# Splitting the last batch's gates from its last step, regrouping the logits as six and two batches, and moving the last splits to VectorE

## Chip, cores and metric

The kernel runs on one core of a Trainium2 chip. The metric is device time in microseconds (us) of one execution, lower is better. Engines are TensorE (PE, with its weight loads PEld), VectorE (DVE), ScalarE (ACT), GpSimd (POOL) and SyncE (SP, which only issues transfers here).

## What is computed

An FFT filter on x of 8 batches, 2496 positions, 256 channels, and then a mixture of 8 experts on its 19968 tokens. Each (token, expert) pair is taken in order of falling logit; a token goes to the first expert that still has room (2496 places each).

```python
X = np.fft.rfft(x, axis=1)
y = np.fft.irfft(X * (filt_r + 1j * filt_i)[None], n=2496, axis=1)
x = y.reshape(8 * 2496, 256)
logits = x @ w_gate                      # 8 experts
for idx in np.argsort(-logits.flatten()):
    tok, e = int(idx) // 8, int(idx) % 8
    if assigned[tok] >= 0 or counts[e] >= cap:
        continue
    assigned[tok] = e; counts[e] += 1
for e in range(8):
    out[assigned == e] = np.maximum(x[assigned == e] @ w1[e], 0) @ w2[e]
```

## The kernel before, in words

**Forward part, batch by batch.** `run` writes a list of steps by hand, each with a slot (ten slots to a batch) and a priority within the slot, sorts it and emits the steps in that order. A scheduler then orders each engine's queue from that: earlier emission goes first where it is ready by the scheduler's own model. `s1` and `s2` are the two forward steps; `s2(b, g, dh)` (L224) multiplies with the filter, two products on VectorE (L235, L236) and the sum on GpSimd (L237, L238), into a tile P. Five groups g make up a batch.

**Two uses of P.** `tr(b, q)` (L240) transposes half a group on TensorE (L248) for the way back to positions, and splits the result in a high part (ScalarE, L269) and a low part (L270, VectorE). For the last batch and q over 4 it only copies the transposed rows to the spare tile `y7` (L250); their split comes later, in `inv1` (L290), with the subtraction on GpSimd. In its odd steps `tr` also multiplies the group with the gate's weights (16 small matmuls, L257) and copies the result to `vs` (L259, one buffer). `inv1(b, q)` (L286) is the first inverse step: six matmuls, a copy and two transfers to `zd` (L298; for the last two batches from ScalarE's queue).

**The logits.** They take a short cut through the inverse, eight columns to a batch. `trv` transposes `vs` and splits it into `Vh` and `Vl` (L276 to L279); `v1(g, b0, b1)` is the first inverse step on the columns of batches b0 to b1 (12 matmuls and a copy, L316 and L318); `v2` makes 22 transposes and copies (L332, L333); `v3` multiplies and copies to `lg` (L342, L344). This is done twice: for batches 0 to 6 together and, once its last group is there, for batch 7. `prep` (L523) makes seven VectorE operations of the logits: maximum, a mask Gm, the best expert, and the indicator matrix A (L534).

**Routing.** `threshold` searches the first expert to fill by counting in 11 rounds. A round is a comparison on VectorE (L550, not in the first round), 11 to 13 count matmuls (L558), three VectorE operations (L566 to L568), one matmul (L571) and a few small operations. After the last round come the places of the tokens, and the indices with which tokens are gathered.

**The way back.** The second inverse step, `inv2_parts` (L376), is done for the first two batches while the forward part runs, and for the other six as 30 units after it. A unit is two or five groups of 256 columns: matmuls (L391), ScalarE copies (L392), one transfer to `xs` (L395). In `emit`, `after` is a generator that interleaves these units with `inv1` of q from 5 to 9 of the last batch; TensorE's queue there is written out in program order, and `Pump` puts the count matmuls between the units by planned costs and due times. The first count (L558) is emitted before the loop. `more_z` and `more_z2` load ahead into tiles that the forward part has freed.

**Experts.** A last copy releases the weights' load (L993, L795); tokens are gathered from `xs` (L811), transposed (L825), and go through two matmul stages per expert (L847, L890). Routing for the later experts is interleaved there.

Of the kernel before, what the change touches and what calls it, by code (L numbers as in the profile page):

```python
# [7 lines left out]
F32, F32R = mybir.dt.float32, mybir.dt.float32r  # L8
# [4 lines left out]
B, N, D, E8, FF = 8, 2496, 256, 8, 1024  # L13

N1, N2, K1, J = 39, 64, 20, 64
G = 22
S = B * G
# [9 lines left out]
V1, V1D, V2, V3, VP, AC = 8, 0.5, 3, 2, -1, 6.5  # L27
# [106 lines left out]
class Fft:  # L134
# [105 lines left out]
    def tr(s, b, q):  # L240

        nc = s.nc
        g, k = q // 2, 2 * (q % 2)
        yt = [s.yt[b, g, dh] for dh in range(2)]
        p = s.ps.tile([128, 2, D], F32, name="pa", tag="c", bufs=4)
        for h in range(2):
            for dh in range(2):
                nc.tensor.transpose(p[:, h, 128*dh:128*dh+128], yt[dh][:, k+h], s.id)  # L248
        if b == B - 1 and q > 4:
            nc.scalar.copy(s.y7b(q), p)  # L250
        else:
            s.split(b, q, p, nc.vector)
        if k:
            p = s.ps.tile([128, 128], F32, name="pv", tag="c", bufs=4)
            for dh in range(2):
                for k in range(4):
                    nc.tensor.matmul(p[32*k:32*k+32], s.gate[:, dh], yt[dh][:, k], start=dh == 0, stop=dh == 1, skip_group_check=True)  # L257
            s.vs[b, g] = s.wp.tile([128, 128], F32, name="vs", bufs=1)
            nc.scalar.copy(s.vs[b, g], p)  # L259

    def y7b(s, q):
        if q == 9 and s.y9 is None:
            s.y9 = s.wp.tile([128, 4, 128], F32, name="P", bufs=NP).rearrange("p k d -> p (k d)")
        y = s.y7[:, 80+512*q:592+512*q] if q < 9 else s.y9
        return y.rearrange("p (k d) -> p k d", d=D)

    def split(s, b, q, v, eng):
        y = s.yd[b, q] = [s.wp.tile([128, 2, D], F32R, name=n, bufs=3) for n in ("yh", "yl")]
# [17 lines left out]
    def inv1(s, b, q):  # L286

        nc = s.nc
        if (b, q) not in s.yd:
            s.split(b, q, s.y7b(q), nc.gpsimd)  # L290
        zt = s.wp.tile([128, 2, D], F32, name="zt", bufs=ZB)
        p = s.ps.tile([128, 2, D], F32, name="pa", tag="c", bufs=4)
        for h in range(2):
            s.inv(p[:, h], 2*q + h, [y[:, h] for y in s.yd[b, q]])
        last = b == B - 1
        (nc.scalar.copy if last else s.cps[q % 2])(zt, p)
        for r in range(2):
            (nc.scalar if b >= B - 2 else nc.sync).dma_start(s.zd[b].rearrange("a n c -> n a c")[:N2, 20*r+2*q:20*r+2*q+2], zt[64*r:64*r+64])  # L298
# [5 lines left out]
    def v1(s, g, b0, b1):  # L304

        nc = s.nc
        if s.y7 is None:
            s.y7 = s.wp.tile([128, K1 * D], F32, name="Y1", tag="Y1", bufs=2)
            nc.gpsimd.memset(s.y7[:72, :2640].rearrange("p (a n) -> p a n", n=3*G)[:, :, N2:], 0.0)
        c = 8 * (b1 - b0)  # L310
        r = slice(64, 64 + c) if b0 else slice(0, c)
        p = s.pt([128, 4, 128], not b0)
        for k in range(4):
            (h, l), (Eh, El) = ([t[:, 4*g+k] for t in ts] for ts in ((s.Vh, s.Vl), s.cE))
            for m, (v, w) in enumerate(((h, Eh), (h, El), (l, Eh))):
                nc.tensor.matmul(p[:c, k], v[:, 8*b0:8*b1], w, start=m == 0, stop=m == 2)  # L316
        z = s.y7[r, :2640].rearrange("p (r k n) -> p k r n", r=2, k=K1)[:, 4*g:4*g+4, :, :N2]
        nc.scalar.copy(z, p[:c].rearrange("p k (r n) -> p k r n", r=2))  # L318

    def v2(s, b0, b1):  # L320

        nc, c = s.nc, 8 * (b1 - b0)
        r = slice(64 if b0 else 0, (64 if b0 else 0) + c)
        s.U = s.zp.tile([120, G, c], F32, name="xo", tag="xo", bufs=2)
        n = 8 if c > 8 else G
        for g0 in range(0, G, n):
            g1 = min(g0 + n, G)
            p = s.pt([128, g1 - g0, c], not b0)
            for g in range(g0, g1):
                a = s.y7[r, g:g+1]  # L330
                z = bass.AP(tensor=a.tensor, offset=a.offset, ap=[list(a.ap[0]), [G, 6 * K1]])
                nc.tensor.transpose(p[:120, g-g0], z, s.id[r, r])  # L332
            nc.vector.tensor_copy(s.U[:, g0:g1], p[:120])  # L333

    def v3(s, b0, b1):

        nc, c = s.nc, 8 * (b1 - b0)
        n = 8 if c > 8 else G
        for g0 in range(0, G, n):
            g1 = min(g0 + n, G)  # L340
            p = s.pt([128, g1 - g0, c], not b0)
            s.lastv = nc.tensor.matmul(p[:120], s.cD, s.U[:, g0:g1], start=True, stop=True).ins  # L342
            with s.tc.issue_after(s.lastq):
                nc.vector.tensor_copy(s.lg[:, b0:b1, g0:g1], p[:117].rearrange("p g (b e) -> p b g e", e=8))  # L344

    def more_z(s, units):

# [50 lines left out]
    def run(s, cp, wp, xp, ps, freed, prep, rest):  # L398
# [11 lines left out]
        for b in range(B):  # L410
            o = 10*b
# [5 lines left out]
            for g in range(5):  # L417
                for dh in range(2):
                    at(o + 2*g + dh, 1, s.s2, b, g, dh)
                at(o + 2*g + 4.5, 3.5, s.trv, b, g)  # L420
            for q in range(10):
                at(o + q + 3, 3, s.tr, b, q)
                if b < B - 1 or q < 2:
# [5 lines left out]
                    at(z, 5, s.inv2, b, t)  # L429
        at(10*B - 9.5, 0, freed)  # L430
        for g in range(5):
            at(10*B - V1 + g*V1D, 3.8, s.v1, g, 0, B - 1)
            at(10*B - 5.2 + 2*g, 3.6, s.v1, g, B - 1, B)
        at(10*B - V2, 3.8, s.v2, 0, B - 1)
        def prep0():
            with s.tc.issue_after(s.lastq):
                prep(0, G * (B - 1))
        at(10*B - 0.9, 3.7, s.v3, 0, B - 1)
        at(10*B - VP, 3.8, prep0)
        def act():  # L440
            s.cps = (s.nc.scalar.copy,) * 2
        at(10*B - AC, 0, act)
# [1 line left out]
            at(10*B - 15, 9, s.load_z, *u)  # L444
        at(10*B - 0.8, 9, s.more_z, rest[3+NZ:9+NZ])
        at(10*B + 2.9, 3.61, s.more_z2, rest[9+NZ:3+NZ+MZ])
        at(10*B + 2.9, 3.6, s.v2, B - 1, B)
        at(10*B + 2.9, 3.62, s.v3, B - 1, B)
        at(10*B + 2.9, 3.64, prep, S - G, S)
        for q in (2, 3, 4):  # L450
            at(10*B + 2.9, 3.7 + 0.01 * q, s.inv1, B - 1, q)
        for e in sorted(ev, key=lambda e: e[:3]):
            e[3](*e[4])

# [6 lines left out]
class Route:  # L461
# [75 lines left out]
    def counts(s, nj, thr, made=False):  # L537


        nc, n = s.nc, s.n  # L540
# [14 lines left out]
        last = (S - 1) // b  # L555
        for k in range(last + 1):
            w = min(b, S - b*k) * n
            nc.tensor.matmul(c[:KL, :w], s.Gm[:, K*k:K*k+KL], s.A[:, b*n*k:b*n*k+w], start=k == 0, stop=k == last, skip_group_check=True)  # L558
        t1 = s.wp.tile([128, 128], F32, name="t1", bufs=2)[:K, :b*n].rearrange("p (e s) -> p e s", s=b)
        D1 = s.wp.tile([128, 8], F32, name="D1", bufs=2)[:K, :n]  # L560
        XT = s.XT[nj].pop(0)
# [350 lines left out]
def emit(tc, i, out):  # L912
    nc = tc.nc
    with ExitStack() as st:
# [67 lines left out]
        with tc.issue_after(f.lastv):  # L982
            while pump.kind != 'X':
                pump.step_main()
        with tc.manual_schedule(engines={mybir.EngineType.PE}):
            while (0, 0) not in pump.tags:
                pump.feed(0.1)
                c = next(units, None)
                pump.feed(c if c else 0.8)
            for c in units:  # L990
                pass
# [18 lines left out]
        n = 0  # L1010
# [110 lines left out]
```

## Time and profile before

| | us |
|---|---|
| median of 3 runs | 1425.95 (1424.56 to 1429.34) |
| profiled execution | 1424.91 |
| its span, first to last instruction | 1423.1 |
| TensorE busy | 1378.7 (97%) |
| VectorE busy | 892.1 (63%) |
| ScalarE busy | 673.4 (47%) |
| GpSimd busy | 486.0 (34%) |
| mean granted clock of TensorE | 0.989 |

A matmul's end is modelled, so a busy TensorE may still be waiting in part; busy time of an engine does not hold its transfer issues. The profile names an instruction by its line, its engine and "out<-in" in the program's tile names: `pv`, `pa`, `rt` are PSUM tiles, `xo` and `Y` hold results of the way back, `zt` and `zd` the first inverse step.

### The profile page before, as it was taken

To read this page: it belongs to the slowest core of one execution; us is meant where nothing else is said; L and a number is where in the kernel's file an instruction comes from. 1 tells how busy PE (TensorE), PEld (TensorE's weight loads), DVE (VectorE), ACT (ScalarE), POOL (GpSimd) and SP (SyncE) were. 2 spreads that over 40 slices of the span, in tenths; PEclk is the share of its full clock that TensorE was granted. 3 is DMA by queue.
4 is the path that set the end of the run, shared out by engine and by line. 5 is a ranking of instruction groups with operands and counts; after the bars stand their busy time and mean duration, and the time that the engine had idled before them with its cause. 6 is when DMAs were issued, how large, how long until landed. Compare 5 with 4: busy or idle time off the path is not lost. (4 is left out here: it accounts for less than half of the span.)

```text
span 1423.1 us, 27225 instructions
## 1 busy us (share of the span) xinstructions
PE 1378.7 (97%) x10338; PEld 1210.5 (85%) x10338; DVE 892.1 (63%) x2548; ACT 673.4 (47%) x1638; POOL 486.0 (34%) x538
## 2 busy tenths in 40 slices
PE   9999999998969999999999999999999999999998
PEld 8898898876538898988889888889898899899988
DVE  5577676775647769658667875876867635423231
ACT  6766666644564246235335534533623635423231
POOL 3443343431034126323422622433433323323312
PEclk9999999999979999999999999999999999999999
DMA  9786675658981022112112212112111321111100
GB/s 376 253 237 179 198 216 137 152 127 241 333 304 57 21 86 77 32 33 94 59 32 82 70 40 82 53 43 98 51 38 49 124 70 51 47 42 51 40 20 29
DMA packets 58701, 153.75 MB, mean 108 GB/s; under 512 B 10954, under 2 KB 32074, under 8 KB 54986
## 3 DMA queue, kind: packets, MB, share of 16 engines
q1 hardware_dynamic: 29920, 70.10, 16.2%
q0 software_dynamic: 18416, 60.37, 13.0%
q10 hardware_dynamic: 10233, 21.53, 4.6%
q8 instruction: 82, 1.34, 0.4%
q14 instruction: 50, 0.40, 0.1%
HBM read 88.32 MB, written 63.70 MB: 107 GB/s over the span
## 5 line engine op out<-in xcount | busy, mean ns | idle before, releaser
L890 PE MATMUL py<-w1h,hl 128*128 128x256 f32 x2496 | 485.8, 287 | 1.0 <-DVE hl L858 0.7
L890 PEld LDWEIGHTS py<-w1h,hl 128*128 128x128 f32 x2496 | 403.0, 191 | 7.2 <-issue 3.2
L890 PE MATMUL py<-w1l,hl 128*128 128x256 f32 (+1 forms) x1280 | 359.6, 283 | 0.0
L901 POOL DMA_INDIRECT out<-y,oid x160 | 168.4, 1052 | 507.5 <-ACT y L900 459.2
L853 ACT ACTIVATE hl<-pz 128x512 fp32r<-128x512 f32 (+1 forms) x320 | 187.1, 587 | 226.7 <-PE pz L847 203.4
L847 PE MATMUL pz<-xo,w0h 128*128 128x512 f32 (+1 forms) x640 | 263.9, 412 | 3.4 <-DVE hl L855 1.8
L855 DVE SCALAR_TENSOR_TENSOR hl<-pz,hl 128x512 fp32r<-128x512 f32 x256 | 175.2, 688 | 144.7 <-ACT hl L853 143.3
L847 PE MATMUL pz<-z,w0h 128*128 128x512 f32 (+1 forms) x640 | 248.7, 389 | 0.0
L847 PE MATMUL pz<-xo,w0l 128*128 128x512 f32 (+1 forms) x640 | 248.4, 388 | 0.0
L890 PEld LDWEIGHTS py<-w1l,hl 128*128 128x128 f32 (+1 forms) x1280 | 241.7, 189 | 1.9
L811 POOL DMA_INDIRECT xg<-xs,xid x160 | 170.1, 1063 | 129.8 <-issue 51.5
L900 ACT COPY y<-py 128x256 f32<-128x256 f32 x152 | 56.6, 372 | 306.3 <-PE py L890 268.0
L847 PEld LDWEIGHTS pz<-xo,w0l 128*128 128x128 f32 x640 | 120.8, 189 | 24.0
L847 PEld LDWEIGHTS pz<-xo,w0h 128*128 128x128 f32 x640 | 121.6, 190 | 22.0 <-DVE hl L855 2.3
L847 PEld LDWEIGHTS pz<-z,w0h 128*128 128x128 f32 x640 | 121.6, 190 | 15.7 <-DVE z L829 0.6
L219 ACT COPY Y<-p 64x240 f32<-64x240 f32 (+1 forms) x302 | 115.2, 381 | 30.4 <-PE p L213 22.4
L237 POOL TENSOR_TENSOR P<-P 128x256 f32<-128x256 f32 x80 | 58.6, 732 | 168.8 <-DVE P L235 168.6
L550 DVE TENSOR_TENSOR Gm<-M,thr 117x1232 bf16<-117x1232 f32 (+2 forms) x80 | 104.4, 1315 | 0.2
L213 PE MATMUL p<-cS,xr 117*128 117x120 f32 x688 | 94.2, 277 | 2.7 <-ACT Y L219 1.5
L213 PEld LDWEIGHTS p<-cS,xr 117*128 117x128 f32 x688 | 86.0, 193 | 6.8 <-ACT Y L219 4.3
L229 PE MATMUL p<-cW,Y 128*128 128x128 f32 x640 | 88.8, 277 | 0.6 <-DVE Q L236 0.6
L229 PEld LDWEIGHTS p<-cW,Y 128*128 128x128 f32 x640 | 80.1, 191 | 5.8 <-issue 3.9
(218 smaller groups left out, 1982.4 us busy)
## 6 DMA issues: line engine op xcount, KB each, us to landing
z<-zd SPq DMA_DIRECT2D x26, 600.0 KB, 5.3
zd<-zt SPq DMA_DIRECT2D x120, 128.0 KB, 2.7
xs<-xo ACTq DMA_DIRECT2D x18, 600.0 KB, 10.0
xr<-x SPq DMA_DIRECT2D x6, 1536.0 KB
xr<-x SPq DMA_DIRECT2D x6, 1216.0 KB, 9.2
zd<-zt ACTq DMA_DIRECT2D x40, 128.0 KB, 3.3
xs<-xo SPq DMA_DIRECT2D x8, 600.0 KB, 6.6
xr<-x SPq DMA_DIRECT2D x8, 512.0 KB, 6.6
```

Of the source, the lines that this page charges most:

```text
L213: s.lastmm = nc.tensor.matmul(p[:, q-q0, :120], xv[:, q-24*h], s.cS1, start=True, stop=True).ins
L219: c = (nc.vector.tensor_copy if (t == 5 if b else cp) else nc.scalar.copy)(dst, src)
L229: nc.tensor.matmul(p[:, k], s.Y1[b][:, 4*g+k, dh*128:dh*128+128], s.cW[:, 4*g+k], start=True, stop=True)
L237: nc.gpsimd.tensor_tensor(P[:, :, :64], P[:, :, :64], P[:, :, 64:], op=OP.subtract)
L550: nc.vector.tensor_tensor(Gm[:, s0:s1, :m], s.M[:, s0:s1].unsqueeze(2).to_broadcast([117, s1 - s0, m]), thr[:117].unsqueeze(1).to_broadcas ...
L811: s.lastg = s.nc.gpsimd.indirect_dma_start(out=xg[:n], out_offset=None, in_=s.xs, in_offset=bass.IndirectOffsetOnAxis(ap=ids[0][:n, t:t+1] ...
L847: nc.tensor.matmul(p[:, :n], w[:, sl], x[:, k, :n], start=m == 0, stop=m == 5)
L853: s.lasta = nc.scalar.activation(h[:, :n], p[:, :n], AF.Relu).ins
L855: s.R.low = nc.vector.scalar_tensor_tensor(l[:, :n], p[:, :n], 0.0, h[:, :n].bitcast(F32), op0=OP.max, op1=OP.subtract).ins
L890: nc.tensor.matmul(p[:a.stop-a.start], hs[g][f][:, a], b[:, 256*f:256*f+256], start=m == 0, stop=m == 8 * len(terms) - 1, skip_group_check ...
L900: s.lasta = nc.scalar.copy(y, p).ins
L901: st = nc.gpsimd.indirect_dma_start(out=out_rows, out_offset=bass.IndirectOffsetOnAxis(ap=ids[1][:w, 4*g+t:4*g+t+1], axis=0), in_=y[:w], i ...
```

## The change

The gates' matmuls and copy leave `tr` and become a step of their own, `gates`. For batches 0 to 6 it is still called in `tr`; for batch 7 it has slots of its own, nearer to `s2`, and three buffers for `vs` in a free part of `y7`; its `trv` follows half a slot later. The logits are grouped as batches 0 to 5 and batches 6 and 7, and all steps of the second group have earlier slots. `v3` copies the first group on ScalarE and waits no longer behind the last `s2`. `prep` of the first group has an earlier slot. `inv1` of q 2 to 4 moves from behind the last logits to ahead of `v2`. The split's subtraction for q from 5 on moves from GpSimd to VectorE, and the splits of q 5, 6 and 7 are emitted right after the last `prep`. The first unit (with `inv1` of q 5) is put behind the first count's last matmul on TensorE.

```diff
@@ in tr, after the split @@
-        if k:
-            p = s.ps.tile([128, 128], F32, name="pv", tag="c", bufs=4)
-            for dh in range(2):
-                for k in range(4):
-                    nc.tensor.matmul(p[32*k:32*k+32], s.gate[:, dh], yt[dh][:, k], start=dh == 0, stop=dh == 1, skip_group_check=True)
+        if k and b < B - 1:
+            s.gates(b, g)
+
+    def gates(s, b, g):
+
+        nc = s.nc
+        p = s.ps.tile([128, 128], F32, name="pv", tag="c", bufs=4)
+        for dh in range(2):
+            for k in range(4):
+                nc.tensor.matmul(p[32*k:32*k+32], s.gate[:, dh], s.yt[b, g, dh][:, k], start=dh == 0, stop=dh == 1, skip_group_check=True)
+        if b < B - 1:
             s.vs[b, g] = s.wp.tile([128, 128], F32, name="vs", bufs=1)
-            nc.scalar.copy(s.vs[b, g], p)
+        else:
+            s.vs[b, g] = s.y7[:, 4688+128*(g%3):4816+128*(g%3)]
+        nc.scalar.copy(s.vs[b, g], p)
 
+    def late_split(s, q):
+        s.split(B - 1, q, s.y7b(q), s.nc.vector)
+
@@ in inv1 @@
-            s.split(b, q, s.y7b(q), nc.gpsimd)
+            s.split(b, q, s.y7b(q), nc.vector)
@@ in v1 @@
-            nc.gpsimd.memset(s.y7[:72, :2640].rearrange("p (a n) -> p a n", n=3*G)[:, :, N2:], 0.0)
+            nc.gpsimd.memset(s.y7[:80, :2640].rearrange("p (a n) -> p a n", n=3*G)[:, :, N2:], 0.0)
@@ in v2 and in v3 @@
-        n = 8 if c > 8 else G
+        n = 8 if c > 16 else G
@@ in v3 @@
-            with s.tc.issue_after(s.lastq):
-                nc.vector.tensor_copy(s.lg[:, b0:b1, g0:g1], p[:117].rearrange("p g (b e) -> p b g e", e=8))
+            (nc.vector.tensor_copy if b0 else nc.scalar.copy)(s.lg[:, b0:b1, g0:g1], p[:117].rearrange("p g (b e) -> p b g e", e=8))
@@ in run @@
-                at(o + 2*g + 4.5, 3.5, s.trv, b, g)
+                if b < B - 1:
+                    at(o + 2*g + 4.5, 3.5, s.trv, b, g)
+                else:
+                    at(o + 2*g + 2.1, 1.5, s.gates, b, g)
+                    at(o + 2*g + 2.6, 1.5, s.trv, b, g)
         for g in range(5):
-            at(10*B - V1 + g*V1D, 3.8, s.v1, g, 0, B - 1)
-            at(10*B - 5.2 + 2*g, 3.6, s.v1, g, B - 1, B)
-        at(10*B - V2, 3.8, s.v2, 0, B - 1)
+            at(10*B - V1 + g*V1D, 3.8, s.v1, g, 0, B - 2)
+            at(10*B - 7 + 2*g, 1.6, s.v1, g, B - 2, B)
+        at(10*B - 4.2, 3.8, s.v2, 0, B - 2)
         def prep0():
             with s.tc.issue_after(s.lastq):
-                prep(0, G * (B - 1))
-        at(10*B - 0.9, 3.7, s.v3, 0, B - 1)
-        at(10*B - VP, 3.8, prep0)
+                prep(0, G * (B - 2))
+        at(10*B - 3.6, 3.8, s.v3, 0, B - 2)
+        at(10*B - 0.9, 3.8, prep0)
@@ further down in run @@
-        at(10*B + 2.9, 3.6, s.v2, B - 1, B)
-        at(10*B + 2.9, 3.62, s.v3, B - 1, B)
-        at(10*B + 2.9, 3.64, prep, S - G, S)
+        at(10*B + 1.2, 3.6, s.v2, B - 2, B)
+        at(10*B + 1.2, 3.62, s.v3, B - 2, B)
+        at(10*B + 1.2, 3.64, prep, S - 2*G, S)
+        for q in (5, 6, 7):
+            at(10*B + 2.9, 3.8, s.late_split, q)
         for q in (2, 3, 4):
-            at(10*B + 2.9, 3.7 + 0.01 * q, s.inv1, B - 1, q)
+            at(10*B + 0.1 + 0.2*q, 5, s.inv1, B - 1, q)
@@ in counts @@
-            nc.tensor.matmul(c[:KL, :w], s.Gm[:, K*k:K*k+KL], s.A[:, b*n*k:b*n*k+w], start=k == 0, stop=k == last, skip_group_check=True)
+            s.lastc = nc.tensor.matmul(c[:KL, :w], s.Gm[:, K*k:K*k+KL], s.A[:, b*n*k:b*n*k+w], start=k == 0, stop=k == last, skip_group_check=True).ins
@@ in emit, after the first count @@
+        with tc.issue_after(R.lastc):
+            next(units)
```

## Rows read from the trace of the kernel before

**Rows 1.** Stretches: length, then busy time of PE, PEld, DVE, ACT, POOL, clock, DMA share, GB/s

```profile
307.85:320.91 13.06, 10.22 (x129) 7.28 (x127) 10.16 (x15) 6.87 (x16) 2.05 (x3) 1.00 0.89 208
320.91:328.55 7.64, 7.21 (x42) 6.98 (x42) 4.38 (x11) 1.21 (x3) 0.69 (x1) 0.55 0.84 202
329.17:341.73 12.56, 9.50 (x58) 6.46 (x56) 8.19 (x22) 6.07 (x13) 5.16 (x4) 1.00 0.77 202
329.17:408.57 79.40, 71.65 (x323) 38.82 (x321) 46.12 (x185) 48.82 (x110) 5.16 (x4) 1.00 0.90 318
418.25:426.79 8.54, 7.60 (x20) 5.02 (x21) 8.24 (x11) 4.82 (x10) 6.53 (x6) 0.50 0.54 189
426.79:1423.10 996.31, 979.99 (x6968) 876.53 (x6966) 613.07 (x1934) 409.37 (x987) 343.26 (x326) 1.00 0.17 56
...
384.00:413.00 29.00, 21.78 (x79) 10.61 (x77) 15.01 (x90) 20.93 (x57) 1.24 (x2) 0.95 0.95 369
```

**Rows 2.** Timeline, end of the way back: start, length, engine, line, shape [idle before]

```profile
407.95 0.62 ACT L392 COPY xo<-pv 120x512 f32<-120x512 f32 x1
...
408.67 0.32 ACTq L395 DMA_DIRECT2D xs<-xo  x1
...
409.77 0.16 DVE L767 SCALAR_TENSOR_TENSOR xid<-ex,js 128x4 int32<-128x4 f32 x1
...
413.71 0.97 POOL L811 DMA_INDIRECT xg<-xs,xid  x1 [2.77 <-DMA xs<-xo]
...
418.25 1.78 PE L825 MATMUL ptr<-id,xg 128*128 128x128 f32 x6 [10.59 <-DMA xg<-xs,xid]
```

**Rows 3.** Timeline, from the last filtered tile to the first count

```profile
312.20 0.73 POOL L238 TENSOR_TENSOR P<-Q 128x256 f32<-128x256 f32 x1
...
317.48 0.65 PE L257 MATMUL pv<-P,gate 128*32 128x128 f32 x16
...
320.91 2.95 PE L332 MATMUL pv<-fid,Y 8*120 8x8 f32 x22 [0.67 <-ACT Y L318]
...
323.90 0.34 DVE L333 COPY xo<-pv 120x176 f32<-120x176 f32 x1 [1.27 <-PE pv L332]
...
324.29 0.94 PE L342 MATMUL pv<-xo,cD 120*120 120x176 f32 x2 [0.43 <-DVE xo L333]
...
324.81 0.64 PE L284 MATMUL pa<-yh,cEh 128*128 128x256 f32 x1
...
325.27 0.34 DVE L344 COPY lg<-pv 117x176 f32<-117x176 f32 x1 [1.03 <-PE pv L342]
...
327.17 1.26 ACTq L298 DMA_DIRECT2D zd<-zt  x2
...
327.49 0.34 DVE L534 TENSOR_TENSOR A<-ar,row 117x176 bf16<-117x176 f32 x1
...
327.99 0.28 PE L284 MATMUL pa<-yh,cEl 128*128 128x256 f32 x1
...
328.35 0.28 PE L284 MATMUL pa<-yh,cEl 128*128 128x256 f32 x1
...
328.56 0.63 PE L558 MATMUL rt<-A,Gm 117*48 117x128 bf16 x8
```

**Rows 4.** Single lines: count, shortest/median/longest ns, first and last start, forms

```profile
L527 DVE TENSOR_REDUCE M<-lg x2: 336/886/1436, 314.1 to 325.6; 117x154 f32<-117x1232 f32 x1, 117x22 f32<-117x176 f32 x1
...
L270 POOL TENSOR_TENSOR yl<-Y,yh x4: 1284/1292/1299, 327.9 to 333.5; 128x512 fp32r<-128x512 f32 x4
...
L805 DVE TENSOR_TENSOR w0l<-wr,w0h x32: 675/684/761, 418.5 to 1200.0; 128x512 fp32r<-128x512 f32 x32
```

**Rows 5.** Timeline of VectorE in the first round, while GpSimd makes the splits

```profile
331.30 1.00 DVE L568 TENSOR_TENSOR X<-D,row 48x24 f16<-48x24 f32 x1
...
333.76 1.02 DVE L586 TENSOR_TENSOR thr<-km,ic 128x7 int32<-128x7 int32 x1
```

**Rows 6.** Waits from 329 to 410: who for whom, us in total, times, longest

```profile
DVE t L566 <- PE rt L558: 14.1, 11, 2.9
```

More of the change, by code (lines that the diff above doesn't have):

```diff
@@ L337, in v3 @@
         nc, c = s.nc, 8 * (b1 - b0)
-        n = 8 if c > 8 else G
+        n = 8 if c > 16 else G
         for g0 in range(0, G, n):
```

## The prediction

> **What bounds the kernel.** I read the page's chain of waits first: from the expert stage to the end it is TensorE on itself. The table by stretches says the same: from 426.79 us on, TensorE is busy 979.99 of 996.31 us at full clock [rows 1]. No line of the change lies there, so the end moves by what the start of that stage moves. That start I followed back in the timeline: the first token transposes come at 418.25, behind the gathers; these wait until 413.71 for the last transfer to `xs`, issued at 408.67 behind the last copy of the way back [rows 2]. The token indices were there at 409.77 [rows 2], so routing ends 3.9 us before it is needed, and the way back sets the end. Its units run from 329.17 to 408.57, with TensorE busy 71.65 of 79.40 us and the transfers 0.90 of the time [rows 1]. VectorE waits 14.1 us in that stage for the count matmuls [rows 6]: routing follows TensorE's queue, and an earlier routing alone is worth little. The stream of units begins behind the first count, at 328.56, and this behind the logits of the last batch [rows 3]. So what matters is when the units start and how freely their first microseconds run.
>
> The sum goes against the profiled execution, 1424.91 us (its span is 1423.1); the median of the runs shown is 1.04 us above it.
>
> **The gates and the order ahead of `v2`.** The last filtered tile is ready at 312.20 + 0.73 = 312.93; its gates come at 317.48 and the 22 transposes of `v2` at 320.91 [rows 3]. That looks like 4.5 us to be had, but TensorE is not idle in between: from 307.85 to 320.91 it is busy 10.22 of 13.06 us [rows 1]. What stood ahead of the gates is only moved, mostly ahead of the last `s2`, which then comes later. What can be won are the gaps, 2.84 us. Into the same stretch come the three inverses of q 2 to 4. These are 18 matmuls; from 327.99 to 328.35 one takes 0.12, so 2.2 us [rows 3]. If all gaps are filled, `v2` starts 0.6 earlier; if the inverses fall behind it and the gaps close, 2.8 or more; if no gap closes, 2.2 later. Each inverse also brings ScalarE a copy and two transfer issues. Two issues take 1.26 us [rows 3], so six take 3.8, queued ahead of the copies for which gates, `trv` and `v1` wait, on an engine busy 6.87 of 13.06 us with the issues not counted [rows 1]. This speaks against more than the small gain; I take 0.6 earlier. SyncE's queue is passed by no step, and the memset on GpSimd only grows by rows.
>
> **From `v2` to the first count, wider by a batch.** The maximum takes 336 ns on 176 elements and 1436 ns on 1232, so 1.04 ns an element [rows 4]: 0.18 us more for a further 176. That holds for five of the seven operations of `prep` and, taken as like it, for the two copies (0.34 each before [rows 3]): 1.3 us, with the two narrow operations 1.4. `v3` takes 0.94 for 176 columns [rows 3]; twice the columns cost between 0.3 and 0.9, I take 0.6. The transposes have 16 rows for 8; I leave their 2.95, with up to 0.5 as the upper end. Together 2.0 later (1.6 to 2.8).
>
> **The inverses no longer block the count.** A is done at 327.49 + 0.34 = 327.83, and the count starts at 328.56 because the last inverse is still in the queue [rows 3]. That gives 0.7 back.
>
> **The count in one piece.** Before, two of the unit's matmuls start at 329.17, between count matmuls, 0.6 behind the count's start. Now the unit waits for all 11. Eight take 0.63 [rows 3], so 11 take 0.9 at the high clock and up to 1.7 at the low one; 1.3 instead of 0.6 is 0.7 later for the units. Routing gains, but has slack.
>
> **The clock.** Before, the granted clock is 0.55 on average from 320.91 to 328.55 [rows 1]. The inverses, which ran in the wait for `prep`, take 3.18 us for the 15 starts from 324.81 to 327.99, 0.21 each, and 0.12 from then on: TensorE is back at 2.4 from 1.2 GHz just before the units [rows 3]. Now nothing is left for that wait of some 5 us, and the units start at the low level. With starts as summed (count at 328.56 - 0.6 + 2.0 - 0.7 = 329.3, units at 330.6) and a rise 3.2 us after work resumes, as before, 1.9 us pass at half speed: 1.0 lost. The lower end is 0; the upper is the second rival.
>
> **The first rounds.** TensorE is idle 12.56 - 9.50 = 3.06 us from 329.17 to 341.73 [rows 1]. Two causes get weaker. GpSimd takes 1.29 us for a split [rows 4], and two small VectorE operations take 1.00 and 1.02 while it runs [rows 5], though X has only 24 columns and a copy of 176 takes 0.34 [rows 3]; VectorE takes 0.68 for the same shape [rows 4]. And ScalarE is full: 6.07 us busy [rows 1], with ten issues of the inverses of q 5 to 9 at 0.63 next to it, an estimate of 12.4 in 12.56. The copies, casts and issues that leave it free room for the units. The new VectorE work, five times 0.68, is 3.4 us; three of the splits can lie in the waits of `v2` and `v3` (1.27 and 1.03 idle [rows 3]), and if all three came between A and the count's result instead, up to 2.0 would fall on routing, under its 3.9. Of the 3.06 I take 2.5 as gained (0 to 3.06). ScalarE's copies of the first group's logits lie ahead of all this, beside a TensorE that was the bound there: nothing, or up to 0.6 for one copy in the way.
>
> **The sum:** -0.6 + 2.0 - 0.7 + 0.7 + 1.0 - 2.5 = -0.1, so **1424.8 us**: no change that shows. About 0.3% (4.3 us) is what a measurement of this kernel can tell from none.
>
> **The rivals.**
>
> *The chain gets ahead.* If the scheduler puts the gates at 312.93 and lets transposes of q 8 and 9 and the inverses fall behind `v2`, `v2` starts 317.48 - 312.93 = 4.5 earlier. The inverses fill the wait for `prep` as before, so the clock is back in time. Then -4.5 + 2.0 - 0.7 + 0.7 - 2.5 = -5.0: 1419.9. For it: the 4.55 us between tile and gates. Against it: the 2.84 us of gaps, and the steps emitted ahead of `v2`. Chance 0.30.
>
> *The clock stays low.* At the start of the expert stage TensorE ran from 418.25 to 426.79 at 0.50 although busy 7.60 of 8.54 us [rows 1]. If it does so behind the empty wait, from 329.3 to 337.8, the units lose half of 7.2 us, 3.6 and not 1.0, and a slower TensorE fills the gaps itself, so that the 2.5 are not gained: -0.6 + 2.0 - 0.7 + 0.7 + 3.6 = +5.0, 1429.9, slower by 0.35%. It decides if TensorE has no other work behind `v3`. For it: the moved inverses were that work. Against it: the rise 3.2 us after 324.81. Chance 0.16.
>
> The Trainium skill, in TensorE: Matmul & The Clock Gate, Part 1, says that the slow state is the default and that activity releases it; by that rule a TensorE that waits through `prep` starts slow, which is this rival's way and would give its 1429.9 if nothing released it sooner. The trace agrees on the two levels (0.50 and 1.00), but also shows the low one with 8-row transposes that count as busy 7.21 of 7.64 us [rows 1].
>
> *The transfers decide.* From 384 to 413 they are busy 0.95 of the time [rows 1]. If that is the limit, what the first rounds gain is lost as a wait for a free `xo` tile: 1424.9. For it: 0.90 over the whole stage. Against it: 0.77 from 329.17 to 341.73, where there is room. Chance 0.10.
>
> **How the numbers follow.** The forecast has 0.44; with the transfers' case no change has 0.54, faster 0.30, slower 0.16. The range takes in both outer cases and the bounds of the gaps and of `prep`: 1418.5 to 1430.5, with some 0.2 left out.
>
> **What would show it.** Right: `v2` of the last two batches within 1 us of 320.3; the last `prep` some 1.2 us longer; TensorE without work for 4 to 5 us ahead of the count; first unit near 330.6 at clock 0.5; VectorE's operation X under 0.34; last copy near 408. Wrong: `v2` before 318, inverses behind it, or a clock that is low beyond 335.

## The result, and the profile after

The changed kernel takes **1437.03 us** (median of 6 runs, 1435.92 to 1441.49) where the kernel before takes 1426.18 beside it: a ratio of 1.0077, 95% interval 1.0062 to 1.0092. That is slower, by 10.9 us, and outside the predicted range. The profiled execution has a span of 1435.4 us, 12.3 more than before.

The expert stage is as it was. The first token transposes of [rows 2] come 11.8 us later, and the 11.8 us are lost in two places: the first unit behind the count starts at 337.67 where it started at 329.17, 8.5 later; and from there to the last copy it takes 82.02 us where it took 78.78, 3.2 more. (Lines have moved: L262 is the gates' multiplication, L309 the store to `zd`, L329 the copy of `v1`, L343 the transposes of `v2`, L550 the matrix A, L574 the count, L401 and L402 a unit's matmul and copy.)

The chain from the gates to the first round, in the timeline of the kernel after (start, length, engine, line, shape, [idle before, and what ended it]; it answers to [rows 3, 5]):

```profile
312.12 1.68 SPq L375 DMA_DIRECT2D F<-zd  x4
...
315.09 0.64 PE L262 MATMUL pv<-P,gate 128*32 128x128 f32 x16
...
317.30 0.60 ACTq L309 DMA_DIRECT2D zd<-zt  x1
317.94 0.62 ACTq L309 DMA_DIRECT2D zd<-zt  x1
...
319.29 0.58 ACTq L309 DMA_DIRECT2D zd<-zt  x1
...
319.91 0.62 ACTq L309 DMA_DIRECT2D zd<-zt  x1
320.15 0.63 ACT L280 CAST yh<-Y 128x512 fp32r<-128x512 f32 x1
...
324.51 3.13 ACTq L309 DMA_DIRECT2D zd<-zt  x2
327.68 0.57 ACT L329 COPY Y<-pv 16x512 f32<-16x512 f32 x1 [6.90 <-DMA F<-zd]
...
328.31 2.96 PE L343 MATMUL pv<-fid,Y 16*120 16x16 f32 x22 [8.17 <-ACT Y L329]
...
336.69 0.52 DVE L550 TENSOR_TENSOR A<-ar,row 117x352 bf16<-117x352 f32 x1
337.26 0.48 PE L574 MATMUL rt<-A,Gm 117*48 117x128 bf16 x3 [2.01 <-DVE A L550]
...
337.67 2.06 PE L401 MATMUL pv<-z,cD 120*120 120x512 f32 x2
...
338.41 0.17 DVE L584 TENSOR_TENSOR X<-D,row 48x24 f16<-48x24 f32 x1
```

The gates come 2.4 us earlier than before, as the change wants it. But ScalarE, free at 320.78, makes the last copy of `v1` only at 327.68. It had 6.90 us of nothing, and the line names what ended them: the load of `F`, an earlier tile for the way back that has nothing to do with `v1`. Ahead of the copy in ScalarE's queue stand the stores of the moved inverses. Four of them went out in 0.6 us each; the last two stand at 324.51 with 3.13 us for both. The waits of this stretch say the same, one behind the other:

```profile
ACT Y L329 <- DMA F<-zd: 6.9, 1, 6.9
...
PE pv L343 <- ACT Y L329: 8.2, 1, 8.2
```

What a store has to do with a load is seen in the program's queues. Each transfer that ScalarE or SyncE issues signals one of eight semaphores (DMAHW0 to DMAHW7), taken in turn by both queues together, and an issue first waits for the earlier transfer on its own. This is from the built program of the kernel after (ScalarE's queue above, SyncE's below):

```
425 L309 DMA zd7_67<-zt_4346 64x2x256 [waits DMAHW6_49,Activation_49]
426 L309 DMA zd7_67<-zt_4346 64x2x256 [waits DMAHW7_49]
427 L329 COPY Y1_3873<-pv_4357 16x4x2x64 [waits PE_49]
...
194 L375 DMA F_4295<-zd3_63 120x512 [waits DMAHW6_49]
195 L375 DMA F_4295<-zd4_64 120x1280 [waits DMAHW7_49]
```

The last two stores take the semaphores on which the third and fourth load of `F`, issued from 312.12 on, are still under way, and an issue that waits holds everything behind it on its engine: here the copy for which the whole chain waits. In the kernel before the same six stores stand behind the last `v1` copy.

What the hold leaves behind, in the table by stretches of the kernel after (columns as in [rows 1]):

```profile
320.00:325.00 5.00, 0.14 (x2) 0.00 (x0) 1.59 (x3) 0.78 (x2) 0.00 (x0) 0.85 0.97 270
325.00:330.00 5.00, 1.69 (x14) 1.69 (x14) 0.00 (x0) 1.16 (x2) 0.00 (x0) 0.50 0.88 270
330.00:335.00 5.00, 4.38 (x25) 3.33 (x25) 2.00 (x5) 0.58 (x1) 0.00 (x0) 0.50 0.01 4
335.00:340.00 5.00, 2.99 (x11) 1.61 (x9) 2.81 (x8) 0.23 (x1) 0.00 (x0) 0.50 0.00 0
337.67:350.23 12.56, 11.26 (x58) 7.68 (x57) 6.27 (x23) 5.12 (x10) 0.00 (x0) 0.89 0.56 161
337.67:419.69 82.02, 73.85 (x320) 40.24 (x319) 45.68 (x187) 46.74 (x106) 0.00 (x0) 0.96 0.86 301
```

From 320 to 330 TensorE has 1.83 us of work in 10, and the granted clock falls to 0.50. From 330 to 340 the transfers stand still (0.01 and 0.00); no unit makes anything to store yet. The units' first 12.56 us run at a clock of 0.89, and the stage as a whole at 0.96, with 73.85 us of work for TensorE where [rows 1] have 71.65.

### The profile page after: what moved, and what is told of

It reads as the page before. It is cut to its first block, busy times and chain, and to the rows that moved or that the text cites. A ratio compares the mean times of both kernels' runs of the same rounds, so it can differ in the third digit from the quotient of the medians.

```text
span 1435.4 us, 27218 instructions
## 1 busy us (share of the span) xinstructions
PE 1381.9 (96%) x10338; PEld 1212.5 (84%) x10338; DVE 891.2 (62%) x2550; ACT 675.0 (47%) x1641; POOL 478.0 (33%) x533
```

## The experiments

They ran on chips of two speeds: on two chips the kernel before takes 1446 us (e1 to e4 on one, e5, e6 and the repeats of the pair on the other), on the others 1426. Ratios are against the kernel before on the same chip; positions in the trace are compared at one speed only. A trace is of one execution: those of e6, e9 and e10 are of the longest of theirs, those of e7, e12 and e14 of the shortest (e6 took 1437.8 to 1448.0 us, e9 1421.4 to 1427.6, e7 1422.2 to 1425.5), so a difference of a microsecond or two between two traces says little by itself. Each line is one run: ratio with its interval, start of `v2`, start of the first unit, TensorE's idle time in the 12.56 us from there (length less busy time), and start of the way back's last copy, in us.

| kernel | ratio | v2 | first unit | idle | last copy |
|---|---|---|---|---|---|
| **chips at 1446:** before | 1 | 320.63 | 328.68 | 3.05 | 410.80 |
| after | 1.0068 (1.0039 to 1.0097) | 329.28 | 338.64 | 0.48 | 420.00 |
| inverses put back (e1) | 0.9996 (0.9983 to 1.0008) | 318.32 | 328.30 | 2.31 | 411.27 |
| their stores by SyncE (e2) | 1.0016 (1.0002 to 1.0029) | 322.08 | 331.44 | 1.32 | 413.89 |
| before, inverses early (e3) | 1.0017 (1.0002 to 1.0032) | 325.82 | 331.17 | 2.60 | 413.29 |
| after, loads by GpSimd (e4) | 1.0032 (1.0019 to 1.0044) | 324.38 | 333.60 | 0.72 | 413.99 |
| their stores behind the copies (e5) | 1.0014 (0.9997 to 1.0031) | 321.53 | 330.73 | 0.70 | 411.08 |
| before, splits by VectorE (e6) | 0.9978 (0.9956 to 1.0000) | 319.05 | 328.24 | 2.26 | 411.97 |
| **chips at 1426:** before | 1 | 320.91 | 329.17 | 3.06 | 407.95 |
| after | 1.0077 (1.0062 to 1.0092) | 328.31 | 337.67 | 1.30 | 419.69 |
| before, tiles turned (e7) | 0.9978 (0.9966 to 0.9990) | 319.42 | 328.60 | 1.68 | 405.27 |
| e1, tiles turned (e8) | 1.0000 (0.9988 to 1.0012) | 319.74 | 329.73 | 2.37 | 407.29 |
| early gates, 7+1, tiles turned (e9) | 0.9979 (0.9967 to 0.9992) | 319.50 | 329.06 | 2.08 | 409.29 |
| before, shorter stores (e10) | 0.9979 (0.9964 to 0.9994) | 324.11 | 332.41 | 1.54 | 411.57 |
| after, stores by GpSimd (e11) | 1.0016 (1.0003 to 1.0028) | 321.72 | 331.08 | 0.49 | 413.33 |
| e7 and e14 together (e12) | 0.9966 (0.9951 to 0.9981) | 319.58 | 327.80 | 1.27 | 403.07 |
| e9, stores by GpSimd (e13) | 0.9976 (0.9960 to 0.9993) | 319.01 | 329.23 | 0.75 | 406.85 |
| e6, stores by GpSimd (e14) | 0.9998 (0.9985 to 1.0011) | 319.94 | 329.13 | 1.27 | 406.31 |

### Which part loses the time

**e1** puts the three inverses back behind the logits and leaves all else of the change:

```diff
-            at(10*B + 0.1 + 0.2*q, 5, s.inv1, B - 1, q)
+            at(10*B + 2.9, 3.7 + 0.01 * q, s.inv1, B - 1, q)
```

> The change with the inverses of q 2 to 4 of the last batch put back behind the last logits, all else as changed. Theory A (ScalarE's queue is held by the inverses' zd stores, which wait for the semaphores of the loads into F, ahead of the last copy of v1): v2 of the last two batches starts at 319 to 321 and not at 328.3, the first unit at 328 to 331, the time is 1422 to 1428, within 0.3% of before. Theory B (the wider last logits and the unbroken count cost by themselves): the first unit at 333 or later, 1430 or more. Theory C (the empty wait ahead of the count and the low clock): no wait is empty here, so as A.

The loss is gone: 0.9996. So it lies in the moved inverses; the grouping, the splits and the order behind the count together cost nothing that shows. In its timeline ScalarE runs without a hold up to `v2`, and the clock is up when the units start (the first takes 1.12 us, not 2.06):

```profile
317.69 0.58 ACT L329 COPY Y<-pv 16x512 f32<-16x512 f32 x1
...
318.32 2.96 PE L343 MATMUL pv<-fid,Y 16*120 16x16 f32 x22 [0.68 <-ACT Y L329]
...
328.30 1.12 PE L401 MATMUL pv<-z,cD 120*120 120x512 f32 x2
...
376.37 1.84 ACT L402 COPY xo<-pv 120x512 f32<-120x512 f32 x4 [6.89 <-DMA xs<-Y]
...
411.27 0.60 ACT L402 COPY xo<-pv 120x512 f32<-120x512 f32 x1
```

**e2** leaves the inverses early and takes only their six stores out of ScalarE's queue:

```diff
-            (nc.scalar if b >= B - 2 else nc.sync).dma_start(s.zd[b].rearrange("a n c -> n a c")[:N2, 20*r+2*q:20*r+2*q+2], zt[64*r:64*r+64])
+            (nc.scalar if b >= B - 2 and not (last and 2 <= q < 5) else nc.sync).dma_start(s.zd[b].rearrange("a n c -> n a c")[:N2, 20*r+2*q:20*r+2*q+2], zt[64*r:64*r+64])
```

> The change with the six zd stores of the inverses q 2 to 4 issued from SyncE's queue; the inverses stay early. Theory A: ScalarE is not held, v2 starts at 319 to 322, and what is left of the loss is that of the empty wait and the low clock: 1424 to 1430. Theory C: the loss stays, 1433 to 1438.

**e4** leaves the stores where they are and takes the loads of `F` and `cW` out of the shared turn, by GpSimd's queue:

```diff
-            s.load_z(*u, z)
+            s.load_z(*u, z, s.nc.gpsimd)
...
```

> The change with the six loads into cW and F issued from GpSimd's queue, which has other semaphores; the inverses stay early and the transfers stay as many. Theory A: the stores wait for no load, ScalarE is not held for more than 1 us, v2 starts at 319 to 322, 1424 to 1430. Rival D (the stores are held because the transfer engines are full, whatever the semaphore): ScalarE is held as before, v2 at 326 or later, 1434 or more.

e2 takes most of the loss away and e4 about half, each from its own side. In e2 the hold moves to SyncE, where the six issues take 6.33 us and only loads stand behind. In e4 the transfers are still 0.97 busy from 320 to 325 us, but the wait of the copy falls from 6.90 to 1.71, and that the profile puts down to issuing (two issues of 1.27 us together stand just ahead). That the transfers are merely full at that time is not the cause. e4 still falls short of what was expected of it: the wait is over 1 us and `v2`, at 324.38, is 2.4 later than the latest start named, so the issues' own length ahead of the copy counts too. First e2, then e4:

```profile
318.23 6.33 SPq L309 DMA_DIRECT2D zd<-zt  x6
...
321.45 0.57 ACT L329 COPY Y<-pv 16x512 f32<-16x512 f32 x1
...
322.08 2.96 PE L343 MATMUL pv<-fid,Y 16*120 16x16 f32 x22 [1.35 <-ACT Y L329]
```

```profile
322.44 1.27 ACTq L309 DMA_DIRECT2D zd<-zt  x2
323.75 0.57 ACT L329 COPY Y<-pv 16x512 f32<-16x512 f32 x1 [1.71 <-issue]
```

**e3** makes the move alone, in the kernel before:

```diff
-            at(10*B + 2.9, 3.7 + 0.01 * q, s.inv1, B - 1, q)
+            at(10*B + 0.1 + 0.2*q, 5, s.inv1, B - 1, q)
```

> The kernel before with one part of the change alone: the inverses of q 2 to 4 in their early slots. Theory A: the stores of q 4 wait for loads into F that land near 324 to 327, and three ScalarE steps of the last logits stand behind them, so v2 starts at 326 to 329 instead of 320.9 and the time is 1431 to 1437. Theory C: only the wait for prep is empty, v2 within 1 us of before, 1426 to 1429.

Here the turn falls differently: the last two stores take the semaphores of the first two loads of `F`, and none of the six issues takes over 0.62 us. The forecast hold did not come. `v2` is 5.2 us later than before's all the same: the copy waits 2.81 us for TensorE, which itself waited 2.53 us for ScalarE's copy of the gates, behind the inverses' casts and other copies, and 1.20 us for VectorE.

```profile
321.83 0.33 PE L276 MATMUL pv<-fid,vs 128*128 128x128 f32 x1 [2.53 <-ACT vs L259]
...
323.92 0.28 PE L316 MATMUL pv<-cEh,Vl 128*8 128x128 f32 x1 [1.20 <-DVE Vl L279]
...
325.20 0.57 ACT L318 COPY Y<-pv 8x512 f32<-8x512 f32 x1 [2.81 <-PE pv L316]
```

The count is not in one piece there, the first unit comes only 2.5 us later, and the loss is 0.17%, not the 0.35% and more that was expected. So the move costs something without any hold, and the 0.7% come only where the turn is unlucky.

### The hold alone, and the same pair on one chip

> The kernel after once more, beside the variants. Every theory: ratio 1.005 to 1.009 against before; the first v1 copy behind the six transfer issues waits 5 to 8 us again, v2 near 328, first unit behind the count near 337.7. If the hold came from chance in the order of the transfers, it would be under 3 us here and the ratio under 1.003.

> The kernel before on the chip of the variants, for its trace. Compared with the variant that puts the inverses back (its unit stage ran from 328.3 to 411.3): theory 'the start is won, the stage gives it back' expects the first unit here at 329 to 330 and the last copy of the way back within 0.5 us of 411.3, so that the stage is 1 us shorter than there. If the inverses' place were all, the first unit would stand at 328.3 here too.

The hold is not chance: on a chip of the other speed the copy waits 7.05 us for `F` again, and the ratio is 1.0068. Beside before's trace at that speed, e1 starts its first unit 0.4 us earlier and ends 0.5 later.

**e5** keeps the inverses early and in ScalarE's queue, but emits their stores behind the last `v1` copy:

```diff
+        if last and 2 <= q < 5:
+            s.held.append((q, zt))
...
+    def held_stores(s):
+        with s.tc.issue_after(s.lastz):
+            while s.held:
+                q, zt = s.held.pop(0)
+                s.store_z(B - 1, q, zt)
...
```

> The change, with the six stores of the inverses of q 2 to 4 behind the last v1 copy in ScalarE's queue; the inverses' matmuls and copies stay ahead of v2, SyncE's queue is untouched. Theory A (the stores' waits held the copies behind them): the wait of 6.9 us ahead of the last v1 copy goes, v2 at 321 to 322.5, ratio 1.001 to 1.003; the stores are still held for some microseconds, but nothing urgent stands behind them. Theory B (the inverses' matmuls and copies ahead of v2 are what costs): v2 at 326 or later, ratio over 1.005. What remains over 1.0000 is the price of the inverses' work in the chain and of the empty wait ahead of the count at 1.2 GHz: 2 to 3 us at the first unit against the variant with the inverses put back.

```profile
320.90 0.58 ACT L343 COPY Y<-pv 16x512 f32<-16x512 f32 x1
320.93 7.45 ACTq L317 DMA_DIRECT2D zd<-zt  x5
...
321.53 2.96 PE L357 MATMUL pv<-fid,Y 16*120 16x16 f32 x22 [1.36 <-ACT Y L343]
...
328.47 0.59 ACT L250 COPY P<-pa 128x512 f32<-128x512 f32 x1 [7.00 <-DMA F<-zd]
...
330.73 1.12 PE L415 MATMUL pv<-z,cD 120*120 120x512 f32 x2
```

This settles which part of the move costs most. The hold is as long as ever, 7.00 us, but what stands behind it now is a copy that nobody needs yet. `v2` starts 7.8 us earlier than in the kernel after on the same chip, the last copy comes 8.9 earlier, and 1.0068 becomes 1.0014.

### Why the freer first rounds bring so little

**e6** puts the late splits on VectorE in the kernel before, three of them behind the last `prep`:

```diff
...
-            s.split(b, q, s.y7b(q), nc.gpsimd)
+            s.split(b, q, s.y7b(q), nc.vector)
...
+        for q in (5, 6, 7):
+            at(10*B + 2.9, 3.8, s.late_split, q)
```

> The kernel before with one part of the change alone: the late splits on VectorE, those of q 5 to 7 right behind the last preparation. The prediction's step (first rounds run freer): X at 0.17 instead of 1.00 us, gaps of TensorE in the first 12.6 us of the unit stage down from 3.1 to about 0.6, last copy of the way back 2 to 3 us earlier, ratio 0.998. Rival (the stage gives the gain back, in the wait for the last stores of the tiles reused, or it is bound by transfers): X as short, first microseconds fuller, but last copy within 0.7 us of before's and ratio 0.9995 to 1.0005.

X falls from 1.20 to 0.17 us, but TensorE's idle time only from 3.05 to 2.26. The last copy comes no earlier in its trace, but that is of e6's longest execution, at a clock of 0.94 in the unit stage (0.98 in before's); the ratio, 0.9956 to 1.0000, doesn't tell. The rest of the idle time stands beside holds, again by `zd` stores, those of q 5 to 9; two lines of the kernel before have one that the prediction passed over:

```profile
337.42 3.57 ACTq L298 DMA_DIRECT2D zd<-zt  x2
341.09 0.58 ACT L392 COPY xo<-pv 120x512 f32<-120x512 f32 x1 [4.56 <-DVE Gm L550]
```

The wait is put down to VectorE's Gm; the issue that took 3.57 us just ahead of the copy is what held it (by the program these two stores wait for the semaphores of the stores of q 4). **e14** is e6 with all stores of the last batch from q 2 on issued by GpSimd, which has nothing else to do then:

```diff
-            (nc.scalar if b >= B - 2 else nc.sync).dma_start(s.zd[b].rearrange("a n c -> n a c")[:N2, 20*r+2*q:20*r+2*q+2], zt[64*r:64*r+64])
+            (nc.gpsimd if last and q > 1 else nc.scalar if b >= B - 2 else nc.sync).dma_start(s.zd[b].rearrange("a n c -> n a c")[:N2, 20*r+2*q:20*r+2*q+2], zt[64*r:64*r+64])
```

> The kernel before with the late splits on VectorE and the zd stores of the last batch from q 2 on issued from GpSimd's queue; the tiles are not turned. Theory A: TensorE idle under 1.3 us in the first 12.6 us of the units (2.26 with the splits alone), longer waits at the tile switch (6 to 8 us for 5), last copy within 1.5 us of before's, ratio 0.998 to 1.000. If the holds are not what leaves TensorE idle there: 2.0 us or more idle.

Idle time falls to 1.27 us, and the stage to 77.18 from 78.78 (before's idle time is 3.05 and 3.06 at the two speeds, so that this may be set beside e6); the ratio stays at 0.9998, and the longer wait at the tile switch that was expected is not there (4.64 us). (How the idle time divides is not firm: e7, below, which leaves splits and stores as they were, has 1.68, with a hold of 3.13 us for 3.57.) First the row of e6, then that of e14:

```profile
328.24:340.80 12.56, 10.30 (x60) 7.11 (x60) 8.60 (x26) 6.45 (x14) 0.00 (x0) 1.00 0.75 202
```

```profile
329.13:341.69 12.56, 11.29 (x72) 8.15 (x72) 8.44 (x26) 7.46 (x15) 6.94 (x12) 0.99 0.73 203
```

**e7** asks where such a gain goes. Result tiles of the units come from a cycle of six: two of one pool, and four in the tile Y. At the 16th unit a new pool opens over Y's memory, and its first tile waits for Y's last store, issued one unit earlier: 4.53 us in before, 5.42 in after (below), 6.89 in e1.

```profile
376.40 1.84 ACT L392 COPY xo<-pv 120x512 f32<-120x512 f32 x4 [4.53 <-DMA xs<-Y]
```

Turned by three, the 16th and 17th unit take the two other tiles:

```diff
-        s.nload = s.nstore = 0
+        s.nload, s.nstore = 0, 3
```

> The kernel before with the cycle of the way back's result tiles turned by three, so that the unit at which the late pool opens takes a tile of another pool and the first late tile comes two units later. The wait of 5.36 us for the last store out of Y at 372 to 378 should go in every theory. Theory 'the tile switch gives the gain back': last copy of the way back 2 to 5 us earlier than 410.8, ratio 0.997 to 0.9985. Theory 'transfers bound the stage': wait gone, but the time turns up again as other waits for stores or loads, last copy within 1 us of 410.8, ratio 0.9995 to 1.0005.

**e8** turns them in e1, and **e12** in e14:

> The change with the inverses put back and the tiles turned by three. In the run with the inverses put back TensorE was 1.9 us of work ahead of before 42.6 us into the unit stage, and lost it at the tile switch (6.89 us waited) and behind it (34.9 us from there to the last copy for 32.9). Theory 'tile switch': last copy at 407 or earlier, ratio against before 0.996 to 0.998, 1 to 2 us better than before with the tiles turned. Theory 'transfers bound the stage': last copy 409.5 to 411.5 and within 0.7 us of before with the tiles turned.

> The kernel before with the late splits on VectorE, the zd stores of the last batch from q 2 on issued from GpSimd's queue, and the tiles turned by three. Theory A and 'tile switch' together: no hold of ScalarE by stores, TensorE idle under 1.3 us in the first 12.6 us of the units, last copy of the way back 2 to 4 us before that of the run with the tiles turned alone, ratio 0.9950 to 0.9970. If the holds are harmless: 0.9978 as with the tiles turned alone.

The stage falls to 76.67 us in e7 (ratio 0.9978) and to 75.27 in e12, by its median the fastest kernel here (0.9966: 0.3% under the kernel before, 1.1% under the kernel after by the two ratios), though the intervals of e7, e9 and e13 overlap with its own. e8, expected at 0.996 to 0.998, shows no gain against before: its first unit is 1.1 us behind e7's, behind the wider `prep` (9.16 us from `v2` to A for 6.59), and it loses 0.9 more on the way, with a hold of 4.37 us by stores for 3.13. The tile switch therefore takes gains back only in part; what else does so in e8 was not tried further. Line by line, the end of the way back: the kernel after (the wait at the tile switch, last copy, last transfer, first token transposes), e7, and e12 as one row by stretches.

```profile
386.31 1.84 ACT L402 COPY xo<-pv 120x512 f32<-120x512 f32 x4 [5.42 <-DMA xs<-Y]
...
419.69 0.60 ACT L402 COPY xo<-pv 120x512 f32<-120x512 f32 x1
420.39 0.32 ACTq L405 DMA_DIRECT2D xs<-xo  x1
...
430.06 1.30 PE L841 MATMUL ptr<-id,xg 128*128 128x128 f32 x5 [10.63 <-DMA xg<-xs,xid]
```

```profile
405.27 0.60 ACT L392 COPY xo<-pv 120x512 f32<-120x512 f32 x1
405.97 0.32 ACTq L395 DMA_DIRECT2D xs<-xo  x1
415.59 1.77 PE L825 MATMUL ptr<-id,xg 128*128 128x128 f32 x6 [10.59 <-DMA xg<-xs,xid]
```

```profile
327.80:403.07 75.27, 71.11 (x323) 38.64 (x321) 46.90 (x189) 47.47 (x109) 7.95 (x14) 1.00 0.92 334
```

**e10** tests whether transfers bound the stage: units store three of five groups (or one of two); rows of batch 0, stored in the forward part, fill the rest, so those tokens are not computed.

```diff
+                if b >= B - NPOST:
+                    w -= 2 if w > 2 else 1
...
```

> The kernel before, but the units after the forward part store only three of five (one of two) groups; what they leave out is filled with rows of batch 0 in the forward part, so those tokens are wrong. 41% of the bytes written in the unit stage are gone, all other instructions stay. Theory 'transfers bound the stage' : stage of 82.1 us (first unit 328.7 to last copy 410.8) falls to 75 to 78, as TensorE has 73.1 us of work, and the wait for the last store out of Y falls below 3. Theory 'TensorE, ScalarE and the order of the queue bound it': 81 to 82.1, ratio 0.9995 or more.

With 41% fewer bytes stored the stage takes 79.16 us, with TensorE busy 73.17 of them; before took 78.78. So transfers do not bound it. The wait at the tile switch falls to 2.83 us, but the stage gains nothing by it. Where the ratio of 0.9979 comes from is not shown: in the trace, of its longest execution, the shorter last store lands sooner, so that the token transposes come 8.07 us behind the last copy (10.30 before), but the added stores put the first unit off by 3.2 us, which clouds the rest.

### What is left of the change

**e11** takes the stores off ScalarE in the change itself, and **e9** and **e13** keep its early gates and VectorE splits with groups of seven and one, inverses put back and tiles turned, without and with the stores by GpSimd:

```diff
...
-        at(10*B + 1.2, 3.6, s.v2, B - 2, B)
+        at(10*B + 1.2, 3.6, s.v2, B - 1, B)
...
```

> The change, with all zd stores of the last batch from q 2 on issued from GpSimd's queue. Theory A (holds of ScalarE by waiting stores): no wait of over 2 us ahead of the last v1 copy, v2 at 321 to 322.5, first unit near 331, and no hold of 2 to 4 us by stores in the first 15 us of the units; ratio against before 0.998 to 1.001. If the holds in the units are harmless: as with the stores behind the copies, 1.001 to 1.002. If GpSimd's issues are slow or its transfers late (a copy waiting for a zt tile): 1.003 or more.

> A candidate: early gates and VectorE splits of the change, groups of seven and one as before, inverses behind the logits, tiles turned by three. v2 near 318, the last preparation as short as before's, so count at 325.5 and first unit near 326.3 instead of 328.7, clock at full level. If an earlier start of the units is worth its length: 2 us better than the change with inverses back and tiles turned, ratio 0.995 to 0.9965. If transfers bound the stage from its start on, the same, as the stores start earlier too; if the floor is in loads that do not move with the units, last copy within 0.7 us of that variant's.

> The candidate with early gates, groups of seven and one and turned tiles, and the zd stores of the last batch from q 2 on issued from GpSimd's queue. If the early gates are worth anything beside this (v2 at 319 instead of 321), 1 us or more better than the variant of before with the same queue and tiles: 0.994 to 0.996. If not, the same as that one within 0.0012.

e11 stays at 1.0016, where e2 and e5 are: without any hold ahead of `v2`, the change still loses 0.16%. By what was expected of e11, that is the case in which the holds inside the unit stage are harmless, as e14's 0.9998 says too. Its units start at 331.08, 1.9 us behind before's, at a clock of 0.86 in the first 12.56 us. e9 (0.9979; expected 0.995 to 0.9965) is no better than e7 without early gates, and e13 (0.9976) no better than e12. So the early gates bring nothing that shows. With them and the inverses put back, `v2` starts at 319.0 to 319.7 (e8, e9, e13); with the gates as before at 319.4 to 320.9 (before, e7, e12, e14).

## Why the prediction was wrong

**The step that failed** is the one on the moved inverses' stores, behind the term -0.6: "Two issues take 1.26 us [rows 3], so six take 3.8, queued ahead of the copies for which gates, `trv` and `v1` wait". The queue was read rightly and the price wrongly. An issue was costed by its own length, as it stands where nothing holds it. What it may have to wait for was not asked, and with it all that stands behind waits too: 6.90 us for one copy. The evidence was there, in the issue of 3.57 us of the kernel before, shown above. So `v2`, forecast 0.6 us earlier, came 7.4 later. Without the hold it starts at 321.5 (e5) and 321.7 (e11), 0.9 and 0.8 later than before's at the same speed, between the "0.6 earlier" that was taken and the "2.2 later" of the case in which no gap closes.

Term by term, as far as the runs show them:

- *Wider `prep`, +2.0.* From the start of `v2` to that of A: 6.58 us before, 8.38 after, so 1.8 (on the other chip 6.59 and 8.38); 2.6 where the inverses stand behind (e1, 9.15). Right.
- *Count no longer blocked (-0.7), and in one piece (+0.7).* From A to the first unit it takes 0.98 us for 1.68: -0.7 together for a forecast of 0. Eight of the 11 matmuls run ahead, on the part of A that was ready early (L574 starts at 334.20), which the sum had not seen.
- *Clock, +1.0.* The units start at 0.50, as forecast, though the wait ahead of the count is not all empty: four transposes and eight count matmuls lie in it, and 2.01 us of nothing. The first 12.56 us at 0.89 cost 1.4, at 0.86 (e5, e11) 1.8, at 0.78 (the kernel after at the other speed) 2.8. The Trainium skill, TensorE: Matmul & The Clock Gate, Part 1, has the slow state as the default; the trace agrees, with 0.50 from 325 to 340.
- *First rounds, -2.5.* Mis-sized, and in part put down to the wrong cause. VectorE's splits give 0.8 (e6); another 1.0 was held by stores (e14), where the prediction said "ScalarE is full". In the kernel after the idle time is 1.30 us, but a slower TensorE fills gaps there, as the second rival said: e1, with the same splits at full clock, has 2.31.
- *The stage* from first unit to last copy should by the last two terms have been 1.5 us shorter, and is 3.2 longer: 2.2 more of work for TensorE, at a clock of 0.96, and 1.0 more of idle time (8.17 for 7.13). Behind the first 12.56 us, for which the sum has no term, the idle time is 6.87 for 4.07. The wait at the tile switch lies there, and behind it the clock falls once more, which it does not in the kernel before (rows by stretches, after and then before):

```profile
377.67:387.67 10.00, 7.22 (x39) 3.97 (x38) 4.80 (x17) 3.21 (x8) 0.00 (x0) 1.00 0.76 288
387.67:397.67 10.00, 10.00 (x34) 4.85 (x33) 5.77 (x18) 5.25 (x11) 0.00 (x0) 0.83 0.87 254
```

```profile
369.17:379.17 10.00, 8.16 (x43) 4.46 (x42) 4.76 (x21) 4.25 (x9) 0.00 (x0) 1.00 0.85 290
379.17:389.17 10.00, 9.94 (x49) 5.26 (x48) 7.35 (x26) 5.48 (x11) 0.00 (x0) 1.00 0.94 295
```

With 7.4, 1.8 and -0.7 the first unit is 8.5 late; with 3.2 in the stage that is 11.7, and the last copy is 11.7 late.

**The rivals.** The second, a clock that stays low, had the right sign and shows in the trace, but its 3.6 us were too much, and it wasn't the cause: e5 has the empty wait too, and loses 0.14%. The first, the chain ahead, comes nearest in e1: `v2` 2.3 us earlier than before's at its speed, and no gain at the end. The third, that transfers decide, is contradicted by e10. **The signs:** X under 0.34 and a first unit at clock 0.5 came, and so did a sign of being wrong, a clock that is low beyond 335. `v2` within 1 us of 320.3, the empty 4 to 5 us, the first unit near 330.6 and the last copy near 408 did not come, and the first of these, seen at 328.31, points at the right place.

## What to carry to other kernels

A transfer issue is an instruction that can wait, and it holds its engine's whole queue (6.90 us here): before one is moved ahead of urgent work, look up which earlier transfer its semaphore still belongs to, on any queue that shares the turn, or put it behind that work or on an engine that has nothing to do. A long issue in the timeline (3 us for two where 1.26 is usual) was such a hold here, whatever name the wait of the next instruction bore. Before a stretch is made faster, look for the wait further on that will take the gain back, here a pool opened over a tile whose last store had just been issued. Turning the tiles (e7, 0.22%) is the one single step here with right results whose interval lies clear of 1; no part of the change by itself has a gain as clear.

## What was not expected of the hardware

Two stores of 128 KB took 3.13 us to issue, and held ScalarE, because their semaphores belonged to loads of up to 600 KB on another engine's queue: 6.90 and 7.05 us for ScalarE on two chips. The same issues by GpSimd, whose transfers use semaphores of their own in the program, took 3.65 us for six (e11) and held no other engine. And the clock of the unit stage differs where the units do the same work, and not by the kernel alone: 1.00 in one trace of the kernel before and 0.98 in the other, 1.00 in e7, e8, e12 and e14, 0.96 in the kernel after, e9 and e13, 0.94 in e11. In the kernel after it falls behind TensorE's wait of 2.71 us at the tile switch. In the kernel before, where that wait is 1.77 us, it stays at 1.00; but in e8 it stays there behind a wait of 2.68, too. Within one kernel it goes with the time: over the whole run e6's five shorter executions (up to 1441.3 us) have a mean clock of 0.986 to 0.991, the five longer ones (from 1446.1) of 0.984 to 0.986. What decides it stays open.
